# Two more y pairs in the key sweep, seven products in three more w2 steps, and another planned order

## The chip, the cores and the metric

The kernel runs on one core of a Trainium2 chip. The metric is the device time of one execution in microseconds (us); lower is better.

## The reference

What is computed, for `x` of 2048 rows by 576 columns (the second block's `B_x` has the same values as `A_x`):

```python
def _A_ref(x, wqkv, wo):                      # linear attention, 32 heads of 18 columns
    q, k, v = split_heads(x @ wqkv)
    phi = lambda t: where(t > 0, t + 1, exp(t)) + 1e-6
    pq, pk = phi(q), phi(k)
    kv = einsum("bhsd,bhse->bhde", pk, v);  z = pk summed over s
    o = (pq @ kv) / (pq . z + 1e-6)
    return merge_heads(o) @ wo

def _B_ref(x, w1, b1, w2, b2):                # 576 -> 4608 -> 576
    y = _layernorm(x, axis=-1)
    h = _gelu(y @ w1 + b1)
    return h @ w2 + b2

g = _sigmoid((x * gate_w).sum(-1, keepdims=True))
return g * _A_ref(x, ...) + (1 - g) * _B_ref(x, ...)
```

All data is float32. The kernel makes each product from a rounded high part and a low part of its operands (three terms: high by high, high by low, low by high).

## The kernel before

The program has three stages, one behind the other on TensorE (PE): a key sweep, the attention, and the two-layer block (called the MLP here).

**Key sweep.** The 2048 rows are 16 tiles of 128, taken in the order `ORDER`; the loop is `for n in range(FIRST, NT)`, and one turn of it is called round n here (3 to 15). In a round PE projects a tile's keys in two halves, into PSUM banks 6 and 7 (`project(i, KEY, half)`), adds the part `add_products(before, 0)` for the tile before, projects the queries in two halves into banks 6 and 7 again (`projected(i, QUERY)`), and adds the part `add_products(before, 1)`. The last three rounds (13 to 15) leave out the queries; those of the first of the three (`late[0]`) come behind the loop. A bank is free again when ScalarE (ACT) has made relu and exp of it (`e<-ps`, `e<-e`) and VectorE (DVE) has put both together: `k<-ps,e` for keys, `acc<-ps,e` (or `accs<-ps,e`) for queries. DVE also makes the low parts: `y<-t,y` for the next tile, `ks<-k,ks` and `xs<-xn,xs` for the sums. These instructions stand in program order on each engine.

**Slots and jobs.** Each round has three slots, 3n, 3n+1 and 3n+2, in which `run(slot)` puts other work into the same in-order queues: slot 3n stands behind `xs<-xn,xs` and ahead of the queries' `acc<-ps,e`, slots 3n+1 and 3n+2 behind these. Two kinds of jobs matter here:

- Gates and moments: in one slot DVE takes the row sums of two tiles (`gates_in`), in the next ACT takes exp and square root (`gates_act`, with two table loads), in the third DVE makes gate and 1/deviation in eight small instructions (`gates_out`) and GpSimd's queue (POOL) writes the two tiles' moments to DRAM (`share_moments`, in the profile `moments<-mr`).
- y pairs: the normalized x of two tiles, with the sums that seven products in place of eight need. `load_pair` reads the pair's moments back, spread over all partitions (`accs<-moments`), and x (`accs<-in_xm`, `accs<-in_xe`), seven issues on SyncE's queue (SP). Four `normal_pair` (`accs<-accs`, 768 wide), four `sum_pair` (384 wide), and four parts of `split_pair` and `split_tails` (an ACT copy, then two DVE instructions, `ys<-...`, the last part `y<-accs,y`) follow, and `store_pair` writes the parts to DRAM (`yd<-ys`). All pairs use one place, `yr` and `rows` in the tile `accs`: a pair is loaded over the one before.

`Y_JOBS` has the slots of each pair: that of the load, of the four normalizations, of the four differences, of the four parts. Before, the first half's four pairs are made so. The second half's four are made in the MLP (`make_y`, tiles `accs` and `ystage`).

**MLP.** The second half's rows follow the first's; each has 18 chunks of 256 of the 4608 columns, so there are 36 steps k. A step has "up" products (y by w1, seven products of seven matmuls, 512 wide) and "down" products (h by w2, 288 wide). For a step in `SEVEN` down is seven products, in 14 units of 6 matmuls; for another it is eight units of 12. Before, steps 0, 6, 13 and 35 are plain. A step in `SEVEN` costs sums ahead of its products: four of h (`u<-u`, 512 wide), four of w2 (`fresh<-fresh`, 288 wide), on DVE or POOL as the set `ON_DVE` says, more low parts (`h<-u,h`, `region<-fresh,region`), and more additions of products to the result (`accs<-ps,accs`).

The order of the MLP's instructions comes from `plan`, which takes each engine's next instruction by due times and costs written into it: `lag`, `late`, `slop` and other numbers of `TUNED`, a duration for each operation, and for PE one duration for every up matmul and one for every down matmul.

## Time and profile before

| | |
|---|---|
| median of 3 runs | 1095.46 us (1095.13 to 1095.92) |
| span of the profiled execution, first to last instruction | 1094.1 us |
| key sweep, up to the sums' last product | 0 to 180.6 us |
| attention | 180.6 to 272.6 us |
| MLP | 272.6 us to the end |
| PE, DVE, ACT, POOL busy | 1087.8, 917.2, 687.5, 235.6 us |

The profile has no time of its own for the profiled execution: its span is 1.36 us below the median of the runs, which also holds what lies ahead of the first and behind the last instruction. All shares are of the span. Nearly all instructions have the line L120, that of the helper which keeps program order, so one goes by tiles and shapes. A matmul's recorded duration holds the way through the array, so that durations of matmuls that follow each other overlap; their rate is read from how many start in a stretch of time. DVE's overlap too, by some 0.08 us each.

### The profile page before, as it was taken

How to read it: one execution, taken by the hardware profiler on the slowest of the kernel's cores; microseconds unless marked ns; L12 is line 12 of the kernel's file. 1: busy time of each engine (PE TensorE's matmuls, PEld its weight loads, DVE VectorE, ACT ScalarE, POOL GpSimd, SP SyncE). 2: the span in 40 equal slices, each digit the busy share in tenths (PEclk: the TensorE clock that was granted, in tenths of full speed). 3: DMA queues.
4: the chain of work that ended last, by engine and by line, in shares of the span. 5: the costliest groups of instructions: out<-in, count | busy, mean ns of one | idle time of the engine just before them, and what ended most of it. 6: DMA issues, size and time to landing. Idle time of an engine off the chain costs nothing.

```text
span 1094.1 us, 18599 instructions
## 1 busy us (share of the span) xinstructions
PE 1087.8 (99%) x6694; PEld 996.8 (91%) x6694; DVE 917.2 (84%) x1553; ACT 687.5 (63%) x1230; POOL 235.6 (22%) x232
## 2 busy tenths in 40 slices
PE   9999999999999999999999999999999999999998
PEld 9999999999898889988889999989899999999898
DVE  4568784895799999899999997988887888878888
ACT  6677765454667887777877876455545555455552
POOL 2111112531123232332111202121122211221110
PEclk9999999999999999999999999999999999999999
DMA  6466772745745565764556559574444435444432
GB/s 186 128 88 190 171 218 102 286 173 188 252 152 195 184 206 192 235 215 161 199 174 222 195 192 395 174 253 119 138 145 118 130 119 150 132 119 119 135 100 87
DMA packets 109006, 189.72 MB, mean 173 GB/s; under 512 B 8940, under 2 KB 68604, under 8 KB 104818
## 3 DMA queue, kind: packets, MB, share of 16 engines
q1 hardware_dynamic: 108002, 187.78, 53.3%
q8 instruction: 53, 0.87, 0.3%
q10 hardware_dynamic: 720, 0.74, 0.2%
q14 instruction: 39, 0.32, 0.1%
q0 software_dynamic: 192, 0.01, 0.1%
HBM read 121.70 MB, written 66.80 MB: 172 GB/s over the span
## 4 chain that ended last, share of the span: by engine, by line
PE 93%; DVE 3%; DMA 1%; ACT 1%; issue 0%; SPq 0%; ACTq 0%; DVEq 0%
PE ps L120 93%; DVE accs L120 1%; DMA s<-in_wm 0%; DVE h L120 0%; DMA fresh<-in_ue 0%; DMA ystage<-late_acc 0%; ACT u L120 0%; DMA s<-in_we 0%; DVE wp L120 0%; DVE region L120 0%; SPq L120 0%; DVE den L120 0%; DVE fresh L120 0%; DVE ystage L120 0%; DVE u L120 0%
## 5 line engine op out<-in xcount | busy, mean ns | idle before, releaser
L120 PEld LDWEIGHTS ps<-region,h 128*128 128x128 f32 x3072 | 437.8, 188 | 30.1 <-ACT ps L120 4.3
L120 PE MATMUL ps<-region,h 128*128 128x288 f32 x3072 | 457.1, 296 | 1.0 <-DVE region L120 0.4
L120 DVE TENSOR_TENSOR accs<-ps,accs 128x576 f32<-128x576 f32 x330 | 246.1, 753 | 60.9 <-PE ps L120 54.1
L120 PE MATMUL ps<-y,wa 128*128 128x512 f32 x1008 | 257.6, 393 | 0.0
L120 PEld LDWEIGHTS ps<-y,wa 128*128 128x128 f32 x1008 | 180.9, 188 | 30.3 <-ACT ps L120 0.2
L120 POOL TENSOR_TENSOR fresh<-fresh 128x288 f32<-128x288 f32 (+1 forms) x128 | 116.4, 913 | 410.5 <-DMA fresh<-in_w 129.6
L120 PE MATMUL ps<-y,wb 128*128 128x512 f32 x756 | 199.3, 394 | 0.1
L120 DVE TENSOR_TENSOR h<-u,h 128x512 fp32r<-128x512 f32 x240 | 165.9, 704 | 8.7 <-ACT u L120 8.7
L120 PEld LDWEIGHTS ps<-y,wb 128*128 128x128 f32 x756 | 133.9, 188 | 20.9 <-ACT u L120 0.5
L120 ACT ACTIVATE region<-fresh 128x576 fp32r<-128x576 f32 (+1 forms) x132 | 81.3, 625 | 73.5 <-PE ps L120 72.9
L120 PE MATMUL ps<-y 128*128 128x288 f32 (+1 forms) x896 | 125.8, 297 | 0.3 <-DVE y L120 0.2
L120 PEld LDWEIGHTS ps<-y 128*128 128x128 f32 x896 | 122.6, 189 | 1.8 <-DVE y L120 0.4
L120 ACT ACTIVATE ps<-ps 128x576 f32<-128x576 f32 (+1 forms) x127 | 78.7, 621 | 45.0 <-PE ps L120 21.5
L120 POOL TENSOR_TENSOR u<-u 128x512 f32<-128x512 f32 x44 | 57.0, 1296 | 193.5 <-DVE h L120 54.9
L120 DVE TENSOR_TENSOR region<-fresh,region 128x576 fp32r<-128x576 f32 (+1 forms) x132 | 93.8, 723 | 1.1 <-ACT region L120 1.1
L120 ACT ACTIVATE u<-ps 128x512 f32<-128x512 f32 x73 | 43.0, 589 | 68.4 <-PE ps L120 68.2
L120 ACT ACTIVATE h<-u 128x512 fp32r<-128x512 f32 x128 | 73.5, 622 | 10.0 <-DVE u L120 5.5
L120 ACT ACTIVATE h<-u,b1s 128x512 fp32r<-128x512 f32 x73 | 52.6, 722 | 42.6 <-DVE u L120 42.4
L120 PE MATMUL ps<-wp,qt 128*128 128x288 f32 x448 | 63.0, 297 | 0.0
L120 DVE TENSOR_TENSOR u<-ps,u 128x512 f32<-128x512 f32 x74 | 50.4, 683 | 13.5 <-PE ps L120 12.7
L120 PEld LDWEIGHTS ps<-wp,qt 128*128 128x128 f32 x448 | 59.8, 188 | 0.0
L120 DVE TENSOR_TENSOR u<-u 128x512 f32<-128x512 f32 x84 | 58.1, 691 | 1.7 <-POOL u L120 1.1
(137 smaller groups left out, 1052.1 us busy)
## 6 DMA issues: line engine op xcount, KB each, us to landing
w1d<-wa SPq DMA_DIRECT2D x17, 1280.0 KB
wa<-w1d SPq DMA_DIRECT2D x68, 320.0 KB
fresh<-in_w SPq DMA_DIRECT2D x70, 288.0 KB
y<-yd SPq DMA_DIRECT2D x14, 1280.0 KB
w1d<-wb SPq DMA_DIRECT2D x17, 960.0 KB
wb<-w1d SPq DMA_DIRECT2D x51, 320.0 KB
yd<-ystage SPq DMA_DIRECT2D x28, 320.0 KB
fresh<-in_um SPq DMA_DIRECT2D x64, 128.0 KB
```

The source lines that it names most:

```text
L120: self.last = self.tc.keep_in_program_order(op(*args, **kwargs))
```

## The change

Four things change.

1. `Y_JOBS` has six pairs: the first half's four, and two of the second half. `load_pair` and the others go to the right half by `divmod(pair, TPB)`. Pairs come every six slots: loads in slots 12, 18, 24, 30, 36 and 41. `MOMENTS` has groups of two tiles up to 12, with `GATES_AT` for their slots. Loads stand behind the other jobs of their slot. The last pair's jobs reach slot 48, behind the loop, and `run(48)` to `run(50)` stand between the last projections and products. `make_y` makes two pairs instead of four.
2. Steps 0, 6 and 13 are in `SEVEN`; step 13 is also in `FIVES`.
3. `ON_DVE` names each sum by itself, and `DVE_SUMS` is gone.
4. `plan` costs matmuls by their place in a run of the same kind (`EACH`), may hold a run of up products up to `hold` matmuls, and has other numbers in `TUNED`.

```diff
-MOMENTS = ((0, 2), (2, 4), (4, 6), (6, 8), (8, 16))
+MOMENTS = ((0, 2), (2, 4), (4, 6), (6, 8), (8, 10), (10, 12), (12, 16))
-Y_JOBS = ((13, (16, 16, 17, 17), (18, 18, 19, 19), (18, 19, 20, 21)), (20, (22, 22, 23, 23), (25, 25, 27, 27), (25, 26, 28, 29)), (27, (31, 31, 32, 32), (33, 33, 34, 34), (34, 35, 35, 36)), (35, (37, 37, 38, 38), (39, 39, 41, 41), (40, 42, 43, 44)))
+Y_JOBS = ((12, (15, 15, 16, 16), (16, 17, 17, 18), (17, 18, 19, 20)), (18, (21, 21, 22, 22), (22, 23, 23, 24), (23, 24, 25, 26)), (24, (27, 27, 28, 28), (28, 29, 29, 30), (29, 30, 31, 32)), (30, (33, 33, 34, 34), (34, 35, 35, 36), (35, 36, 37, 38)), (36, (39, 39, 40, 40), (40, 41, 41, 42), (41, 42, 43, 44)), (41, (44, 44, 45, 45), (45, 46, 46, 47), (46, 47, 47, 48)))
+GATES_AT = (9, 13, 19, 25, 31, 37)
-SEVEN = set([1, 2, 3, 4, 5, 7, 8, ...
+SEVEN = set([0, 1, 2, 3, 4, 5, 6, 7, 8, ...
-    for b, n in enumerate((9, 13, 22, 28)):
+    for b, n in enumerate(GATES_AT):
...
-    for j, (loaded, normal, added, parts) in enumerate(Y_JOBS):
-        at(loaded, load_pair, 0, j)
+    for pair, (loaded, normal, added, parts) in enumerate(Y_JOBS):
+        sup, j = divmod(pair, TPB)
         for n, when in enumerate(normal):
...
+    for pair, (loaded, *_) in enumerate(Y_JOBS):
+        at(loaded, load_pair, *divmod(pair, TPB))
...
     projected(late[0], QUERY)
+    run(3 * NT)
     queries_out(late[0])
     moments_of(end)
+    run(3 * NT + 1)
     for part in range(2):
         add_products(end, part)
+    run(3 * NT + 2)
...
+    EACH = {"up": (226.8, (6.3, 9.3, -2.7, 4.3, 9.3, 1.5, 5.5, 4.2)), "down": (131.9, (0, 3, -1, -2, 7, 1, 2, 3, -6, 1, 0, 1))}
...
-        own = ((what, k, m) in ON_DVE) != ((m, k < NCHUNK) in DVE_SUMS)
+        own = (what, k, m) in ON_DVE
...
-        for j in range(TPB):
+        for j in range(len(Y_JOBS) - TPB, TPB):
             dma(lambda j=j: load_pair(1, j), raw_free["rows"], [("yraw", j)], 5600, 7, each=700)
...
-                        if tb <= ta + 100:
+                        if tb <= ta + 100 and not (run[0] == "up" and run[1] < hold and behind < wait and ta <= free[PE]):
```

What this does to the order, at three places. First DVE in round 11, from the end of the low parts to the queries of the round. Before: two differences (384 wide) stand ahead of the two `acc_101<-ps,e` that free banks 6 and 7.

```order
L120 SCALAR_TENSOR_TENSOR k<-ps,e 128x288
L120 SCALAR_TENSOR_TENSOR ks<-k,ks 128x576
L120 TENSOR_TENSOR xs<-xn,xs 128x512
L120 TENSOR_TENSOR xs<-xn,xs 128x64
L120 TENSOR_TENSOR accs<-accs 128x384 x2
L120 SCALAR_TENSOR_TENSOR acc_101<-ps,e 128x288 x2
L120 TENSOR_TENSOR accs<-accs 128x384 x2
```

The same place now, where the eight instructions of `gates_out` are followed by two normalizations:

```order
L120 TENSOR_TENSOR xs<-xn,xs 128x64
L120 TENSOR_SCALAR g<-g 128x2
L120 RECIPROCAL g<-g 128x2
L120 TENSOR_SCALAR omg<-g 128x2
L120 RECIPROCAL mr_114<-mr_114 128x2
L120 TENSOR_TENSOR mt<-mr_114 128x2
L120 TENSOR_TENSOR mt<-mt 128x2
L120 TENSOR_SCALAR mt<-mt 128x2
L120 TENSOR_TENSOR mr_114<-mr_114,mt 128x2
L120 TENSOR_TENSOR accs<-accs 128x768 x2
L120 SCALAR_TENSOR_TENSOR acc_101<-ps,e 128x288 x2
L120 TENSOR_TENSOR accs<-accs 128x768 x2
```

Gates and normalizations of one round now meet ahead of the queries' instructions; rounds 5, 7 and 9 have the same form.

Second, DVE at the end of the sweep, rounds 14 and 15. Before, from the low parts of round 14 on (`ys` and `y` are parts of the fourth pair, the row `k<-ps,e x2` is the keys of round 15):

```order
L120 TENSOR_TENSOR xs<-xn,xs 128x64
L120 TENSOR_TENSOR ys_561<-accs,ys_561 128x2x256
L120 SCALAR_TENSOR_TENSOR ys_561<-ys_561,low_rows,accs 128x2x128
L120 TENSOR_TENSOR ys_562<-accs,ys_562 128x2x256
L120 SCALAR_TENSOR_TENSOR ys_562<-ys_562,low_rows,accs 128x2x128
L120 TENSOR_TENSOR y<-accs,y 128x256
L120 SCALAR_TENSOR_TENSOR y<-y,low_rows,accs 128x128
L120 SCALAR_TENSOR_TENSOR k<-ps,e 128x288 x2
L120 SCALAR_TENSOR_TENSOR ks<-k,ks 128x576
L120 TENSOR_TENSOR xs<-xn,xs 128x512
L120 TENSOR_TENSOR xs<-xn,xs 128x64
L120 SCALAR_TENSOR_TENSOR acc_102<-ps,e 128x288 x2
```

Now the same stretch holds the fourth difference and three parts of the fifth pair, and the first two normalizations of the sixth, ahead of the keys of round 15:

```order
L120 TENSOR_TENSOR accs<-accs 128x384
L120 TENSOR_TENSOR ys_565<-accs,ys_565 128x2x256
L120 SCALAR_TENSOR_TENSOR ys_565<-ys_565,low_rows,accs 128x2x128
L120 TENSOR_TENSOR ys_566<-accs,ys_566 128x2x256
L120 SCALAR_TENSOR_TENSOR ys_566<-ys_566,low_rows,accs 128x2x128
L120 TENSOR_TENSOR y<-accs,y 128x256
L120 SCALAR_TENSOR_TENSOR y<-y,low_rows,accs 128x128
L120 TENSOR_TENSOR accs<-accs 128x768 x2
L120 SCALAR_TENSOR_TENSOR k<-ps,e 128x288 x2
L120 SCALAR_TENSOR_TENSOR ks<-k,ks 128x576
L120 TENSOR_TENSOR xs<-xn,xs 128x512
L120 TENSOR_TENSOR xs<-xn,xs 128x64
```

And between these low parts and `acc_102<-ps,e`, the queries behind the loop, which stood next to each other, there are now the rest of the sixth pair's jobs:

```order
L120 TENSOR_TENSOR accs<-accs 128x768 x2
L120 TENSOR_TENSOR accs<-accs 128x384 x3
L120 TENSOR_TENSOR ys_564<-accs,ys_564 128x2x256
L120 SCALAR_TENSOR_TENSOR ys_564<-ys_564,low_rows,accs 128x2x128
L120 TENSOR_TENSOR accs<-accs 128x384
L120 TENSOR_TENSOR ys_565<-accs,ys_565 128x2x256
L120 SCALAR_TENSOR_TENSOR ys_565<-ys_565,low_rows,accs 128x2x128
L120 TENSOR_TENSOR ys_566<-accs,ys_566 128x2x256
L120 SCALAR_TENSOR_TENSOR ys_566<-ys_566,low_rows,accs 128x2x128
L120 TENSOR_TENSOR y<-accs,y 128x256
L120 SCALAR_TENSOR_TENSOR y<-y,low_rows,accs 128x128
L120 SCALAR_TENSOR_TENSOR acc_102<-ps,e 128x288 x2
```

Third, PE where the down products begin (step 0, `ps<-region,h`, between up products `ps<-y,wa` and `ps<-y,wb`). Before:

```order
L120 MATMUL ps<-y,wa 128x512 x28
L120 MATMUL ps<-region,h 128x288 x12
L120 MATMUL ps<-y,wb 128x512 x7
L120 MATMUL ps<-region,h 128x288 x24
L120 MATMUL ps<-y,wb 128x512 x7
```

Now:

```order
L120 MATMUL ps<-y,wa 128x512 x28
L120 MATMUL ps<-y,wb 128x512 x4
L120 MATMUL ps<-region,h 128x288 x6
L120 MATMUL ps<-y,wb 128x512 x3
L120 MATMUL ps<-region,h 128x288 x6
L120 MATMUL ps<-y,wb 128x512 x11
```

Step 0's units are of 6 matmuls now. Over the whole MLP the down matmuls go from 3072 to 3036, and the runs of up matmuls between them from 298 to 281.

More of the change, by code (lines that the diff above doesn't have):

```diff
@@ L557, in tile_gated_mix @@
     y_stages.append(y_place.rearrange("p (m s n) -> p m s n", m=2, s=5))
-    jobs = {n: [] for n in range(3 * NT)}
+    jobs = {n: [] for n in range(3 * NT + 3)}
     def at(n, f, *args):
@@ L1418, in tile_gated_mix, with plan @@
     assert len(in_order) == len(ops)
-    def plan(lag, late, slop, slack, guard, ahead, second=None):
-        second = second or (lag, late, slop, slack, guard, ahead)
+    def plan(lag, late, slop, slack, guard, ahead, second, hold, wait):
         slot, due = {o: n for n, o in enumerate(ups)}, {}
@@ L1444, in plan, with streams @@
         port_at, moved, landed = {e: 0 for e in port_until}, 0.0, []
-        next_up, next_down, shift = 0, 0, 0.0
+        next_up, next_down, shift, run = 0, 0, 0.0, ["", 0]
+        def streams(o):
+            n = round(o.ns / (231.7 if o.by[0] == "up" else 132.3))
+            each, more = EACH[o.by[0]]
+            at_ = run[1] if run[0] == o.by[0] else 0
+            return n, n * each + sum(more[at_:at_ + n])
         def offer(o):
@@ L1523, in plan @@
             s, _, o = min(picks, key=lambda x: x[:2])
-            e, t = o.engine, s + o.tail
+            e, t, ns = o.engine, s + o.tail, o.ns
             if e == PE:
+                n, ns = streams(o)
+                t += ns - o.ns
+                run[:] = o.by[0], n + (run[1] if run[0] == o.by[0] else 0)
                 shift = s - nominal[o]
@@ L1530, in plan @@
                         late, slop, slack, guard = second[1:5]
+                        hold, wait = second[6:8]
                 else:
@@ L1553, in plan @@
             else:
-                free[e] = s + o.ns
+                free[e] = s + ns
             if o.port:
```

23 lines of the change are left out of this document (11 added, 12 removed).

## The prediction

> **What bounds the kernel now.** The page comes first: span, busy time, chain.
>
> ```profile
> span 1094.1 us, 18599 instructions
> ...
> PE 1087.8 (99%) x6694; PEld 996.8 (91%) x6694; DVE 917.2 (84%) x1553; ACT 687.5 (63%) x1230; POOL 235.6 (22%) x232
> ...
> PE 93%; DVE 3%; DMA 1%; ACT 1%; issue 0%; SPq 0%; ACTq 0%; DVEq 0%
> ```
>
> PE is busy 1087.8 of 1094.1 us and makes 93% of the chain. What the change takes from PE's work comes off the time, unless PE starts to wait for something that now hides under it. So the next view is busy time by stretch: rounds 10, 12 and 14 of the key sweep, and the tail from the late queries to the sums' last product. Columns: stretch, its length, then busy us (and instructions) of PE, PE's weight loads, DVE, ACT and POOL, the granted clock, the DMA share, GB/s.
>
> ```profile
> 117.12:128.32 11.20, 11.20 (x77) 10.76 (x75) 7.24 (x21) 9.29 (x21) 1.78 (x2) 1.00 0.85 254
> ...
> 139.52:150.72 11.20, 11.20 (x77) 10.76 (x75) 9.03 (x20) 7.89 (x18) 1.44 (x1) 1.00 0.82 217
> ...
> 158.20:165.68 7.48, 7.48 (x49) 7.05 (x47) 6.57 (x14) 5.20 (x13) 1.44 (x1) 1.00 0.70 222
> ...
> 173.16:180.61 7.45, 7.45 (x48) 7.03 (x47) 3.46 (x9) 2.47 (x6) 0.00 (x0) 1.00 0.00 2
> ```
>
> PE is busy for the whole of each stretch: a full round takes 11.20 us, one without queries 7.48. DVE works 6.6 to 9.0 us of these, so it has room on the average, but it works in order, and PE's next step needs certain DVE instructions at certain times. PE's own rows give the two times that matter at the sweep's end: the late queries begin at 173.16, the sums' product at 180.61.
>
> ```profile
> 165.68 3.90 PE L120 MATMUL ps<-y 128*128 128x288 f32 x28
> ...
> 173.16 3.88 PE L120 MATMUL ps<-y 128*128 128x288 f32 x28
> ...
> 180.61 1.13 PE L120 MATMUL ps<-pks,ones 128*128 128x288 f32 x4
> ```
>
> In a full round, PE's next keys need bank 6 back, which is the first `acc<-ps,e` of the queries. Round 10 (from 117.12) shows how near that is. Columns: start, time taken, operation; a count at the end joins neighbours.
>
> ```profile
> 125.52 0.82 DVE L120 TENSOR_TENSOR xs<-xn,xs 128x512 fp32r<-128x512 f32 x2
> 126.26 0.16 DVE L120 TENSOR_SCALAR g<-g 128x2 f32<-128x2 f32 x1
> ...
> 127.52 0.16 DVE L120 TENSOR_TENSOR mr<-mr,mt 128x2 f32<-128x2 f32 x1
> 127.59 0.82 DVE L120 SCALAR_TENSOR_TENSOR acc<-ps,e 128x288 f32<-128x288 f32 x2
> 128.33 3.80 DVE L120 TENSOR_TENSOR accs<-accs 128x768 f32<-128x768 f32 x4
> ```
>
> The low parts `xs` end at 126.34, 9.2 us after the round's start; `gates_out` takes 1.33 us (126.26 to 127.59), and the first `acc<-ps,e` ends some 0.46 us later, 128.05. The next round starts at 128.32: 0.27 us are left. The four normalizations of this round (3.80 us, 0.95 each) stand behind the queries.
>
> **Part 1: the jobs of rounds 5, 7, 9 and 11.** Now `gates_out` and two normalizations meet ahead of the queries' `acc<-ps,e`. Where `xs` ends without pair work ahead of it is seen in round 12, with the sweep's end behind it:
>
> ```profile
> 147.08 0.81 DVE L120 TENSOR_TENSOR xs<-xn,xs 128x512 fp32r<-128x512 f32 x2
> ...
> 157.12 1.23 DVE L120 SCALAR_TENSOR_TENSOR ks<-k,ks 128x576 fp32r<-128x576 f32 x1 [0.96 <-ACT ks L120]
> 158.27 0.81 DVE L120 TENSOR_TENSOR xs<-xn,xs 128x512 fp32r<-128x512 f32 x2
> 159.00 1.14 DVE L120 TENSOR_TENSOR accs<-accs 128x384 f32<-128x384 f32 x2
> 160.06 0.68 DVE L120 TENSOR_TENSOR ys<-accs,ys 128x512 fp32r<-128x512 f32 x1
> 160.66 0.48 DVE L120 SCALAR_TENSOR_TENSOR ys<-ys,low_rows,accs 128x256 fp32r<-128x256 f32 x1
> 161.06 1.14 DVE L120 TENSOR_TENSOR accs<-accs 128x384 f32<-128x384 f32 x2
> ```
>
> Round 12 starts at 139.52 and its `xs` ends at 147.89, 8.4 us on. Round 5 has no pair work of the round before ahead of it, so it is like that: 8.4 + 1.3 + 1.9 + 0.46 = 12.1 us, and PE wants the bank at 11.2: 0.9 late. Rounds 7, 9 and 11 have a pair's last part ahead, as round 10 had: 9.2 + 1.3 + 1.9 + 0.46 = 12.8, 1.6 late each. Sum 0.9 + 3 x 1.6 = 5.7 us. At the lower end the low parts come no later than in round 12 everywhere and it is 3.6; if ACT's two further pairs of table loads come on top, up to 7. I take 5.7, since the round with the same work ahead gave 9.2. Rounds 6, 8, 10 and 12 hold a difference (0.57) and a part (1.0) there: 9.2 + 1.6 + 0.46 = 11.3 at worst, against 11.2; I add nothing.
>
> **Part 2: the sixth pair.** Its moments and load are next; the rows are the write of moments (median from issue to landing at the end), a pair's load on SP's queue, and a load and the instruction that waited for it.
>
> ```profile
> moments<-mr POOLq DMA_DIRECT2D x4, 2.0 KB, 10.6
> ...
> 138.61 0.33 SPq L120 DMA_DIRECT2D accs<-moments  x1
> 140.79 0.58 SPq L120 DMA_DIRECT2D accs<-in_xm  x1
> ...
> 143.41 1.12 SPq L120 DMA_DIRECT2D accs<-in_xe  x2
> ...
> 265.74 0.56 SPq L120 DMA_DIRECT2D accs<-in_ue  x1
> ...
> 269.86 2.10 POOL L120 TENSOR_TENSOR accs<-accs 128x384 f32<-128x384 f32 x2 [21.81 <-DMA accs<-in_ue]
> ```
>
> Rounds 13, 14 and 15 now begin 5.7 later, at 156.4, 163.9 and 171.4. `gates_out` of the sixth pair's tiles stands in slot 39, ends at 156.4 + 9.2 + 1.3 = 166.9, and POOL writes the moments at 167.0. They land 10.6 us later, 177.6. SP waits for that, then issues seven transfers at 0.56 to 0.58 each, the last at 181.2. A load issued at 265.74 was there for its reader at 269.86, 4.1 us later; so all has landed at 185.3. Queued behind on SP are the low copy of x for round 15 and the stores `yd<-ys`; nobody waits for these next.
>
> Who waits is seen from the order: the load stands in slot 41, and the fifth pair's fourth difference and last three parts in slots 42 to 44 read places that the load writes. They wait for it, and being in order they hold up everything behind them on ACT and DVE: the `e<-ps` and `k<-ps,e` of round 15. From 185.3: ACT's copy of a part 0.83, then DVE's two instructions for two parts (0.6 + 0.4 each, from 160.06 to 161.06), 2.0, the small part 0.6, two normalizations 1.9, and the first `k<-ps,e` 0.46: bank 6 is free at 191.1. PE would be ready for the late queries at 173.16 + 5.7 = 178.9, and waits up to 12 us, whole or in part already at round 15's keys; the sum needs only that the bank comes at 191.1.
>
> Behind that the queue goes on: second `k<-ps,e` 0.4, the wait of `ks` for ACT 0.96 (row 157.12), `ks` 1.15, `xs` 0.75, two normalizations 1.9, three differences 1.7 (0.57 each), a part 1.0, the fourth difference 0.5, two parts 2.0, the small one 0.6, and only then `accs<-ps,e` of the late queries, 0.46. Sum 11.4: 202.5. The sums' product needs that bank. PE meanwhile makes the queries (3.9 us from 191.1) and the last products (3.6, from 173.16 to 180.61 less the queries), is done at 198.6 and waits a second time, 4 us. The sums' product moves from 180.61 to 202.5, +21.8 us with part 1 in it. Everything after it is the same attention, so this goes to the end in full.
>
> The DMA price is the widest. If the moments landed at once, the load would still wait until DVE has done the reads ahead of it, about 9.2 us into round 14 (173.1), and have landed at 173.1 + 3.6 + 4.1 = 180.8: 4.5 us less. The trace's 10.6 us is the median of four such writes from this queue in this same sweep, so I take it. The Trainium skill, "DMA: Bandwidth & Descriptors", section "Anatomy of one DMA — SWDGE (gpsimd) path", puts a transfer from that queue at about 2.0 us plus its bytes; by it the sweep would lose 4.5 us less and the total be an estimated 1108, but the trace's 10.6 us for 2 KB contradicts it here.
>
> **Part 3: the MLP.** Rows: PE in a stretch of down products alone; the clock behind the last matmul; the first half.
>
> ```profile
> 1076.00:1088.00 12.00, 12.00 (x92) 1.00 0.27 100
> ...
> 1092.60:1094.10 1.50, 0.00 (x0) 0.50 0.00 0
> ...
> 294.00:646.00 352.00, 351.21 (x2078) 315.37 (x2078) 338.25 (x566) 270.72 (x448) 87.92 (x82) 1.00 0.56 192
> ```
>
> 92 down matmuls start in 12 us: 12/91 = 0.132 us each. There are 3072 - 3036 = 36 fewer, -4.75 us. Seventeen fewer changes between up and down products, at a hundredth of a microsecond, -0.2. In return DVE and POOL get work, priced by these groups (columns: instructions, busy us, mean ns, idle before):
>
> ```profile
> L120 DVE TENSOR_TENSOR accs<-ps,accs 128x576 f32<-128x576 f32 x330 | 246.1, 753 | 60.9 <-PE ps L120 54.1 <-ACT u L120 3.4
> L120 DVE TENSOR_TENSOR h<-u,h 128x512 fp32r<-128x512 f32 x240 | 165.9, 704 | 8.7 <-ACT u L120 8.7
> L120 DVE TENSOR_TENSOR region<-fresh,region 128x576 fp32r<-128x576 f32 x101 | 79.8, 792 | 1.1 <-ACT region L120 1.1
> L120 DVE TENSOR_TENSOR u<-u 128x512 f32<-128x512 f32 x84 | 58.1, 691 | 1.7 <-POOL u L120 1.1
> ...
> L120 DVE TENSOR_TENSOR accs<-accs 128x768 f32<-128x768 f32 x32 | 29.9, 951 | 0.4
> ...
> L120 DVE TENSOR_TENSOR accs<-accs 128x384 f32<-128x384 f32 x32 | 18.5, 577 | 0.3
> ...
> L120 DVE TENSOR_TENSOR fresh<-fresh 128x288 f32<-128x288 f32 x32 | 15.4, 480 | 0.0
> ...
> L120 DVE TENSOR_TENSOR ystage<-accs,ystage 128x256 fp32r<-128x256 f32 x28 | 11.7, 416 | 0.0
> L120 DVE SCALAR_TENSOR_TENSOR ystage<-ystage,low_rows,accs 128x128 fp32r<-128x128 f32 x28 | 11.0, 394 | 2.6 <-ACT ystage L120 2.6
> ```
>
> In the first half DVE gains 14 evictions (10.5 us), 9 low parts of h (6.3), three of w2 at 792 and three at about 480 (3.8), and with the new sharing 4 sums of h (2.8), 5 of w2 (2.4), 3 of w1 (577, 1.7): 27.5. It loses two y pairs: 8 x 951 + 8 x 577 + 14 x (416 + 394) = 23.6. Net +3.9 us. In 294 to 646 DVE is busy 338.25 of 352.00, so it would be at 342 of 347; PE still has more. I cost this at nothing: PE hides it, with 5 us of room; if that is gone, see the third rival. The y pairs' loads leave SP's queue there too, which can only help. The new due times I also cost at nothing either way: PE is busy 351.21 of 352.00 before, so better order can give at most 0.8 in this stretch.
>
> **Sum.** 1094.1 + 21.8 - 4.75 - 0.2 = 1110.95 of span; outside the span lie 1095.46 - 1094.1 = 1.36 us; 1112.3, forecast 1112.
>
> **Rivals.**
>
> *The clock falls at the second wait.* The row from 1092.60 has a granted clock of 0.50, about 2 us after the last matmul. The first wait (10 us or more) is long enough for that; queries and products at half rate would take up to 3.9 us more, which is just the second wait, so it costs nothing. But the second wait of 4 us would then end with attention at half rate: 1 to 5 us, take 2.5: about 1115. The Trainium skill, "TensorE: Matmul & The Clock Gate", Part 1, says that the clock comes back only after some 3.4 us of busy matmuls; by it, half that time is lost at each return. The row at the end agrees that it falls; no row here shows how it comes back in the middle of the kernel.
>
> *The sweep loses less.* Part 1 absorbed (DVE waits less where it starts late): 21.8 - 5.7 = 16.1, 1106.5. Or the moments land quickly: 4.5 less, 1108.
>
> *DVE becomes the bound in the MLP.* If DVE can't use its 13.75 us of idle time in 294:646, since it waits there for products, the stretch would take 352 + 3.9 in place of 352 - 4.8: 8.7 more at worst, 1121; half of it 1116.5. For it: 96% busy. Against: most idle ahead of `accs<-ps,accs` is released by PE.
>
> *The sweep hides the pairs: faster.* DVE has 2 to 4 us free in each round, and if the last load landed before its readers' turn, only 4.95 us of PE's work would be left to count: 1090.5. This decides at one place: the load must be there by about 174, when the fifth pair's fourth difference has its turn, some 7 us after `gates_out` ends at 166.9. The rows say 10.6 + 3.6 + 4.1 = 18.3 us. Part 1 must vanish too.
>
> *Nothing changes:* gain and loss would have to be equal, a loss in the sweep of 5 us.
>
> **How the numbers follow.** The sum as worked out has 0.55 (1109 to 1114.5); the clock 0.15 (about 1115); a smaller loss 0.14 (1106 to 1108); DVE in the MLP 0.06 (1116.5 to 1121); hidden 0.08 (1090.5); equal 0.02. The range 1103.5 to 1118 holds the first three, 0.84 with a share of the fourth, and takes in the ends of part 1 and of the moments together (1112.3 - 2.1 - 4.5 = 1105.7; 1112.3 + 1.3 and the clock's 2.5 to 4: 1118). Faster by over 0.2%: 0.08; within 0.2% (2.2 us, about what a measurement of this kernel can tell from no change): 0.02; slower: 0.90.
>
> **What the profile after would show.** The sums' product `ps<-pks,ones` begins at about 202 and not 181; PE waits 0.9 to 1.6 us at the ends of rounds 5, 7, 9 and 11 for DVE; 10 to 12 us idle on PE ahead of the late queries, with DVE and ACT idle until the sixth load (`accs<-in_xe`) has landed at about 185; a second idle time of about 4 us before the sums' product. From there to the end the length falls by 5 us, from 913.5 to about 908.5, with PE as busy as before. A granted clock below 1.00 behind 202 shows the first rival, DVE without idle time in the MLP's first half and PE below 99% there the third. The forecast is wrong if the moments' write lands in 2 to 4 us, if the last pair's readers don't wait for its load, or if rounds 5 to 11 keep 11.2 us.

## The result and the profile after

The changed kernel takes 1123.85 us (median of 4 runs, 1123.2 to 1124.49) against 1095.69: ratio 1.0252, 95% interval 1.024 to 1.0264. It is slower by 28.2 us, where 16.5 were forecast, and lies 5.9 us above the range.

The page of the changed kernel:

```profile
span 1121.5 us, 18636 instructions
...
PE 1091.6 (97%) x6658; PEld 994.6 (89%) x6658; DVE 957.6 (85%) x1612; ACT 703.6 (63%) x1249; POOL 252.0 (22%) x238
...
PE 71%; DVE 4%; DMA 3%; ACT 1%; issue 1%; SPq 0%; DVEq 0%; ACTq 0%
```

PE's work is 3.8 us more than before (1091.6 for 1087.8), although it has 36 matmuls less: matmuls at a lower clock count as busy for longer (28 of them 5.54, 5.24 and 6.69 us for 3.9 in three of the rows below). 29.9 us of the span are without PE work; PE's share of the chain falls from 93% to 71%. PE's rows show where (start, duration, operation, count; in brackets the idle time ahead and what ended it). Each is the beginning of a round's keys, or of the late queries (200.40), the last is the sums' product:

```profile
61.71 3.90 PE L120 MATMUL ps<-y 128*128 128x288 f32 x28
...
74.30 4.00 PE L120 MATMUL ps<-y 128*128 128x288 f32 x28 [1.22 <-DVE accs L120]
...
85.67 4.01 PE L120 MATMUL ps<-y 128*128 128x288 f32 x28
...
99.30 5.54 PE L120 MATMUL ps<-y 128*128 128x288 f32 x28 [2.04 <-DVE accs L120]
...
125.05 4.00 PE L120 MATMUL ps<-y 128*128 128x288 f32 x28 [1.55 <-DVE acc L120]
...
150.04 4.00 PE L120 MATMUL ps<-y 128*128 128x288 f32 x28 [2.08 <-DVE acc L120]
...
161.41 4.00 PE L120 MATMUL ps<-y 128*128 128x288 f32 x28
...
179.77 5.24 PE L120 MATMUL ps<-y 128*128 128x288 f32 x28 [3.14 <-DVE k L120]
...
200.40 6.69 PE L120 MATMUL ps<-y 128*128 128x288 f32 x28 [11.64 <-DVE k L120]
...
211.83 1.21 PE L120 MATMUL ps<-pks,ones 128*128 128x288 f32 x4 [0.96 <-DVE acc L120]
```

The losses stand in four places. From the program's start to round 5 the two executions differ by 0.6 us (61.71 for 61.12). Rounds 5 to 12 take 99.7 us (61.71 to 161.41) for 89.6: 10.1 more. From round 13 to the late queries it is 38.99 (161.41 to 200.40) for 22.44: 16.55 more. From there to the sums' product 11.43 for 7.45: 4.0 more. Together the sums' product comes 31.2 us later (211.83 for 180.61). From it to the end the kernel takes 909.7 us for 913.5: 3.8 less.

Stretches of the same kernel (columns as in the prediction: round 7, round 8, round 15 with its wait, and the MLP's first half):

```profile
85.67:99.30 13.63, 11.59 (x77) 10.61 (x76) 9.46 (x27) 9.80 (x22) 2.20 (x2) 1.00 0.92 289
99.30:112.14 12.84, 12.84 (x75) 12.40 (x76) 11.11 (x24) 8.13 (x19) 1.42 (x1) 0.87 0.37 81
179.77:200.40 20.63, 8.99 (x48) 8.21 (x48) 8.66 (x17) 5.69 (x13) 1.41 (x1) 0.75 0.51 153
...
304.00:690.00 386.00, 385.49 (x2239) 343.15 (x2238) 375.12 (x605) 298.76 (x494) 105.70 (x103) 1.00 0.55 186
```

In round 8 (99.30) the granted clock is 0.87, and DVE works 11.11 of 12.84 us. In the stretch of 179.77 to 200.40, which is round 15 and the wait behind it, no engine is busy for half of the time. In the MLP's first half PE is busy 385.49 of 386.00 us.

### The profile page after: what moved, and what is told of

The parts are those of the page before. It is cut to its first block, busy times and chain, and to the rows that moved or that the text cites. A ratio compares the mean times of both kernels' runs of the same rounds, so it can differ in the third digit from the quotient of the medians.

```text
span 1121.5 us, 18636 instructions
## 1 busy us (share of the span) xinstructions
PE 1091.6 (97%) x6658; PEld 994.6 (89%) x6658; DVE 957.6 (85%) x1612; ACT 703.6 (63%) x1249; POOL 252.0 (22%) x238
## 4 chain that ended last, share of the span: by engine, by line
PE 71%; DVE 4%; DMA 3%; ACT 1%; issue 1%; SPq 0%; DVEq 0%; ACTq 0%
PE ps L120 71%; DMA y<-yd 1%; DVE accs L120 1%; DMA accs<-late_acc 1%; DVE h L120 1%; DMA fresh<-in_ue 1%; DMA fresh<-in_w 1%; SPq L120 0%; ACT h L120 0%; DMA yd<-ystage 0%; DVE u L120 0%; DVE region L120 0%; DVE wa L120 0%; ACT ps L120 0%; DVE wp L120 0%
## 5 line engine op out<-in xcount | busy, mean ns | idle before, releaser
L120 PEld LDWEIGHTS ps<-region,h 128*128 128x128 f32 x3036 | 430.3, 188 | 30.2 <-ACT ps L120 5.1
L120 PE MATMUL ps<-region,h 128*128 128x288 f32 x3036 | 449.6, 295 | 0.6 <-ACT ps L120 0.4
L120 DVE TENSOR_TENSOR accs<-ps,accs 128x576 f32<-128x576 f32 x344 | 252.6, 752 | 37.6 <-PE ps L120 32.6
L120 DVE TENSOR_TENSOR h<-u,h 128x512 fp32r<-128x512 f32 x249 | 179.1, 746 | 10.2 <-ACT u L120 9.9
L120 POOL TENSOR_TENSOR u<-u 128x512 f32<-128x512 f32 x73 | 98.0, 1343 | 286.7 <-DVE h L120 108.9
L120 POOL TENSOR_TENSOR fresh<-fresh 128x288 f32<-128x288 f32 (+1 forms) x103 | 90.0, 877 | 299.0 <-DVE h L120 89.1
L120 PE MATMUL ps<-y 128*128 128x288 f32 (+1 forms) x896 | 132.4, 306 | 23.0 <-DVE k L120 14.8
L120 PEld LDWEIGHTS ps<-y,wb 128*128 128x128 f32 x756 | 133.9, 188 | 21.6 <-issue 0.6
L120 ACT ACTIVATE ps<-ps 128x512 f32<-128x512 f32 (+1 forms) x135 | 84.0, 624 | 56.6 <-PE ps L120 37.6
L120 ACT ACTIVATE h<-u 128x512 fp32r<-128x512 f32 x140 | 82.0, 620 | 5.7 <-DVE u L120 3.9
L120 DVE TENSOR_TENSOR accs<-accs 128x768 f32<-128x768 f32 (+1 forms) x64 | 49.0, 766 | 9.5 <-DMA accs<-in_xe 8.2
```

Source lines behind the costliest of these rows:

```text
L120: self.last = self.tc.keep_in_program_order(op(*args, **kwargs))
```

## The experiments

In a table first; the times are medians, each compared with runs of the kernel before on the same chip.

| kernel | us | ratio to before, 95% interval | sums' product at, us |
|---|---|---|---|
| changed | 1123.85 | 1.024 to 1.0264 | 211.8 |
| e1_old_sweep | 1121.89 | 1.0219 to 1.0247 | 182.0 |
| e2_new_sweep | 1126.43 | 1.0262 to 1.029 | 211.0 |
| e3_five_pairs | 1115.75 | 1.017 to 1.0198 | 193.8 |
| e4_load_42 | 1118.58 | 1.0189 to 1.0217 | 207.6 |
| e5_share_sp | 1126.40 | 1.0254 to 1.0291 | 216.0 |
| e6_normals_behind | 1123.00 | 1.0228 to 1.026 | 210.3 |
| e7_gates_early | 1129.48 | 1.0286 to 1.0338 | 216.8 |
| e8_seven_only | 1131.06 | 1.0303 to 1.0335 | 182.7 |
| e9_half_normals | 1115.95 | 1.016 to 1.019 | 205.1 |
| e10_no_sixth_write | 1115.32 | 1.0156 to 1.019 | 204.3 |
| e11_write_later | 1121.49 | 1.0216 to 1.0247 | 210.3 |
| e12_old_sweep_light | 1121.09 | 1.0203 to 1.0249 | 181.0 |
| e13_new_order | 1105.11 | 1.0062 to 1.0096 | 181.7 |

### Sweep or MLP: e1, e2, e3

```diff
 e1_old_sweep, against the changed kernel
-MOMENTS = ... (6, 8), (8, 10), (10, 12), (12, 16))
+MOMENTS = ... (6, 8), (8, 16))
+Y_JOBS = (the four pairs of before)
-GATES_AT = (9, 13, 19, 25, 31, 37)
+GATES_AT = (9, 13, 22, 28)
```

> The changed kernel with the key sweep of before (its Y_JOBS, gates and groups of moments: four pairs in the sweep, four in the MLP); SEVEN, ON_DVE and the planner stay as changed. Theory 1 (all of the loss is made in the sweep, and the MLP gains by itself): 1095.7 - 3.8 = 1091.9 us, since from the sums' product to the end the changed kernel took 909.7 us against 913.5. Theory 2 (the seven products in steps 0, 6 and 13 need the two pairs out of the MLP, DVE being near its limit there): DVE gets 23.6 us back in the first half, where it had 11 us of idle time (375.1 busy of 386.0), so up to 12 us later: 1093 to 1104 us, with DVE busy over 98% from 304 to 690.

Measured 1121.89 us. The sweep's loss was gone (sums' product at 182.0), and the MLP was 31 us longer than in the changed kernel (940.9 us from there to the end in the profiled execution, which took 1124.65 us; by the medians it is 28 us). Neither number fits: the loss is larger than the missing room on DVE. This is taken up again with e8, e12 and e13.

```diff
 e2_new_sweep, against the kernel before
 + Y_JOBS, GATES_AT, MOMENTS, run(48) to run(50), make_y of the changed kernel
```

> The kernel before with the changed key sweep alone (six pairs there, two in the MLP); SEVEN, ON_DVE and the planner as before. Theory 1: the sums' product at about 211.8 us as in the changed kernel, and the MLP as before less nothing: 1095.7 + 31.2 = 1126.9 us. Rival (PE waits in the MLP for DVE, 4.2 us in all, and two pairs fewer there take those waits away): down to 1122.7 us.

1126.43 us, the sums' product at 211.0, and 913.3 us from there to the end, as before. So the sweep's loss belongs to the new sweep alone, and two pairs fewer in the old MLP bring nothing.

```diff
 e3_five_pairs, against the changed kernel
-Y_JOBS = (..., (36, ...), (41, ...))
+Y_JOBS = (..., (36, ...))
-GATES_AT = (9, 13, 19, 25, 31, 37)
+GATES_AT = (9, 13, 19, 25, 31)
```

> The changed kernel without the sixth pair in the sweep: five pairs there, three in the MLP. Theory 1 (two separate losses: 10.1 us in rounds 5 to 12, 21.1 us by the sixth pair's load, which the queue of DVE and ACT waits for): the sums' product at 180.6 + 10.1 = 190.7 us, and 1123.9 - 21.1 = 1102.8 us. Rival (DVE has too much work in the sweep, and each of the two new pairs costs the like): half of the loss, 15.6 us, goes: 1108.3 us. In both the MLP may lose up to 1 us by the third pair.

1115.75 us. The sweep did nearly what theory 1 said: the sums' product at 193.8 (190.7 expected), 18.0 us earlier. But the MLP with a third pair took 923.3 us in the profiled execution, 13.6 more than the changed one, and not up to 1. That execution (1118.91 us) lies 3.2 us above the median, so by the medians it is some 10 us. I had taken the MLP for free there too.

### Rounds 5 to 12: e6 and e9

```diff
 e6_normals_behind, against the changed kernel (first four pairs)
-(15, 15, 16, 16) (21, 21, 22, 22) (27, 27, 28, 28) (33, 33, 34, 34)
+(16, 16, 16, 16) (22, 22, 22, 22) (28, 28, 28, 28) (34, 34, 34, 34)
```

> The changed kernel with the first two normalizations of the first four pairs one slot later (16, 22, 28, 34 for 15, 21, 27, 33), behind the queries' acc<-ps,e. Theory A, that of the prediction (two normalizations, 1.95 us, stand ahead of the instruction that frees bank 6, and this sets the loss of each round): each of the four losses of 1.4 to 2.4 us gets smaller by up to 1.95: 7 us less, and the 1.6 us of the halved clock go too: about 1115.5 us. Theory B (DVE and ACT have no idle time from gates_in to the keys' instructions of the next round, so that the time is set by the sum of their work and not by its order): PE begins the next keys earlier and waits ahead of the next queries instead: 1123.9 us, or 1122 if the clock stays up with the shorter waits.

1123.00 us: theory B. PE's rows of the keys of round 8, its queries, and the keys of round 10 (start, duration, idle time ahead):

```profile
97.61 4.00 PE L120 MATMUL ps<-y 128*128 128x288 f32 x28
...
104.83 3.97 PE L120 MATMUL ps<-y 128*128 128x288 f32 x28 [1.47 <-DVE k L120]
...
122.50 4.00 PE L120 MATMUL ps<-y 128*128 128x288 f32 x28
```

The wait ahead of the keys has become one of 1.47 us ahead of the queries, where bank 6 must be freed by the keys' `k<-ps,e`. Two rounds (97.61 to 122.50) take 24.9 us, as in the changed kernel (125.05 to 150.04: 25.0). Only the order had changed.

```diff
 e9_half_normals, against the changed kernel
     def normal_pair(sup, j, a, k):
+        if sup == 0 and k == 1:
+            return
```

> The changed kernel without the second of each two normalizations (the multiplication) of the first four pairs: 8 instructions of 0.95 us left out, one ahead of the queries' acc<-ps,e and one behind it in each pair's rounds. Theory A (in rounds 5 to 12 DVE's work as a whole, with what it must wait for ACT, is longer than PE's: two rounds take 24.9 to 25.8 us where PE needs 22.4): each two rounds get shorter by the 1.9 us that DVE has less, 4 x 1.9 = 7.6 us, and the halved clock of round 8 (1.6) goes with the shorter waits: 1114.7 to 1116.3 us. Theory B (only what stands ahead of acc<-ps,e counts): 4 x 0.95 = 3.8 us, 1120.1 us. Theory C (ACT's table loads set the loss): 1123.9 us.

1115.95 us, theory A. The keys of rounds 6, 8 and 10:

```profile
73.68 4.01 PE L120 MATMUL ps<-y 128*128 128x288 f32 x28 [0.22 <-DVE accs L120]
...
96.96 4.01 PE L120 MATMUL ps<-y 128*128 128x288 f32 x28 [0.61 <-DVE accs L120]
...
120.17 4.01 PE L120 MATMUL ps<-y 128*128 128x288 f32 x28 [0.55 <-DVE acc L120]
```

Two rounds now take 23.2 to 23.3 us for 25.0 to 25.8: 1.7 us less or more, where DVE has 1.9 us less to do. Rounds 5 to 12 lose because DVE, with the waits for ACT that its order holds, has more to do than PE: a pair now comes every two rounds, where before there was one every seven or eight slots. Rounds 11 and 12 of the changed kernel show it (the stretch, then what DVE waits for in it: us, times, longest):

```profile
136.42:161.41 24.99, 22.91 (x151) 21.27 (x151) 19.83 (x46) 17.89 (x39) 3.62 (x3) 1.00 0.64 186
...
DVE y L120 <- ACT y L120: 2.7, 1, 2.7
DVE ks L120 <- ACT ks L120: 1.8, 2, 1.0
```

DVE is busy 19.83 of 24.99 us and waits 4.7 us for ACT (a third wait is 0.2 us), and never for PE.

### The sixth pair: e4, e10, e5

The chain in the changed kernel, on POOL, SP, DVE and ACT; the last row is a stretch, with DMA share and GB/s at its end:

```profile
172.94 0.77 POOL L120 DMA_DIRECT2D moments<-mr  x1 [3.00 <-DVE mr L120]
...
185.00 0.36 SPq L120 DMA_DIRECT2D accs<-moments  x1
...
187.96 1.85 SPq L120 DMA_DIRECT2D accs<-in_xe  x2
...
192.01 0.56 DVE L120 TENSOR_TENSOR accs<-accs 128x384 f32<-128x384 f32 x1 [8.23 <-DMA accs<-in_xe]
...
199.89 0.82 DVE L120 SCALAR_TENSOR_TENSOR k<-ps,e 128x288 f32<-128x288 f32 x2
...
194.55 1.58 ACT L120 ACTIVATE ys<-accs 128x768 fp32r<-128x768 f32 x2 [12.32 <-DMA accs<-in_xe]
...
178.00:185.00 7.00, 5.23 (x29) 5.26 (x30) 4.94 (x10) 1.89 (x4) 1.41 (x1) 0.76 0.03 4
```

The write is issued at 172.94, the load's first transfer at 185.00 (12.06 us later), its last two from 187.96; DVE's fourth difference has what it needs at 192.01, ACT's copy of a part, which reads the last transfers, at 194.55; `k<-ps,e` follows at 199.89, PE at 200.40. In the last 7 us of the 12 the queues move 4 GB/s: most of this time is not transfer, and what passes in it the trace doesn't show.

```diff
 e4_load_42, against the changed kernel
-(41, (44, 44, 45, 45), ...)
+(42, (44, 44, 45, 45), ...)
```

> The changed kernel with the load of the sixth pair one slot later (42 for 41), behind the fifth pair's fourth difference and second part, so that these and the parts after them don't wait for it. The load is issued at the same time, since it waits for the moments (issued 172.94, read from 185.00). Theory 1: the first instructions that wait are then the two first normalizations, which need four of the seven transfers, landed at about 189.8; keys' bank free at 189.8 + 1.9 + 0.5 = 192.2 and not 200.4, 8.2 us earlier: 1115.7 us. Rival (whatever waits first, the whole queue stands until all seven have landed at 192.0): 192.0 + 1.9 + 0.5 = 194.4, 6 us earlier: 1117.9 us. If the wait on PE is not by this load at all: 1123.9 us.

```profile
186.42 0.33 SPq L120 DMA_DIRECT2D accs<-moments  x1
...
193.81 1.95 DVE L120 TENSOR_TENSOR accs<-accs 128x768 f32<-128x768 f32 x2 [5.66 <-DMA accs<-in_xe]
...
196.18 6.50 PE L120 MATMUL ps<-y 128*128 128x288 f32 x28 [6.97 <-DVE k L120]
```

1118.58 us, 5.3 less; the late queries began at 196.18, 4.2 earlier. The two normalizations were the first to wait, as theory 1 said, but the load began 1.4 us later (186.42 for 185.00) and the first transfers were there only at 193.81, 7.4 us after its start, so that the rival's 194.4 for the late queries is the nearer number. What waits first is worth 4 us; whether the write makes the rest is the question of e10.

```diff
 e10_no_sixth_write, against the changed kernel
     def share_moments(b):
+        if b == 5:
+            return
 (load_pair: the sixth pair reads the fifth pair's moments)
```

> The changed kernel without the write of the sixth pair's moments; its load reads the fifth pair's in their place (so the sixth pair is normalized with wrong numbers) and waits for no write. The write was issued at 172.94 and read from 185.00 in the changed kernel, 172.61 and 184.25 with SP's queue. Theory A (the load waits for that write, and all from the load to the sums' product waits for the load): the load starts when its place has been read, at 179.3, 5.7 us earlier: 1123.9 - 5.7 = 1118.2 us, or a little less, as no write is under way meanwhile. Theory B (the load is late for another reason, x or a store ahead of it on SP): 1123.9 us.

```profile
176.54 0.36 SPq L120 DMA_DIRECT2D accs<-moments  x1
...
181.43 1.11 SPq L120 DMA_DIRECT2D accs<-in_xe  x2
...
192.85 5.51 PE L120 MATMUL ps<-y 128*128 128x288 f32 x28 [3.81 <-DVE k L120]
```

1115.32 us: theory A. The load starts at 176.54 for 185.00, as soon as the first of its places is free, its last two transfers go out from 181.43 for 187.96, 6.5 us earlier, the late queries begin at 192.85, 7.5 earlier, and the time falls by 8.5. That is more than the 5.7 expected: x's transfers begin 6.5 us earlier (178.92 for 185.45), are issued in 3.6 us for 4.4 and are there 0.3 us sooner behind the last issue. The other 0.8 us lie between the profiled executions (7.7 us apart in span) and the medians.

```diff
 e5_share_sp, against the changed kernel
-        pool.dma_start(moments[b]...
+        (sp if b == 5 else pool).dma_start(moments[b]...
```

> The changed kernel with the sixth pair's moments written by SP's queue and not by POOL's; the slots are the same. In the changed kernel this write was issued at 172.94 us, and what reads it at 185.00. Theory A (the 12 us are a cost of POOL's queue): on SP the write lands within some 3 us, the load then waits for the reads ahead of it only, which end at 179.3, and everything from the load on comes 5.7 us earlier: 1123.9 - 5.7 = 1118.2 us. Theory B (a write of 512 pieces of 4 bytes takes this long from any queue): 1123.9 us, and if SP's queue stands meanwhile, its loads and stores are late too: up to 1126.

```profile
172.61 0.36 SPq L120 DMA_DIRECT2D moments<-mr  x1
...
184.25 0.36 SPq L120 DMA_DIRECT2D accs<-moments  x1
```

1126.40 us, theory B: from SP's queue the write was issued at 172.61 and its reader went on at 184.25, 11.6 us later. The Trainium skill, "SBUF — State Buffer", section "Who interferes with whom", says that a transfer of POOL's queue that seems held up by DVE is short of descriptors, and that this disappears with another queue. Here it stayed (11.6 us for 12.06): it isn't POOL's queue but the write. The kernel is 2.5 us slower than the changed one, as the load took longer: one issue on SP took 3.94 us (from 186.94), and the last two transfers left from 191.32 for 187.96. Why that issue took so long is not shown.

### The write holds up others: e7 and e11

```diff
 e7_gates_early, against the changed kernel
-GATES_AT = (9, 13, 19, 25, 31, 37)
+GATES_AT = (9, 12, 18, 24, 30, 37)
```

> The changed kernel with the gates of the second to fifth pair of tiles one slot earlier (12, 18, 24, 30 for 13, 19, 25, 31), so that ACT's two table loads (3.2 us with what belongs to them) stand ahead of the second part's products and not right ahead of the next keys' e<-ps, and gates_out stands at the end of the even round and not with the normalizations. Theory A (in the changed kernel ACT's gates_act, which waits for gates_in, holds up the keys' e<-ps by 1.2 to 2 us in rounds 5, 7, 9 and 11, and all of DVE behind it): the loss of rounds 5 to 12 falls from 10.1 to about 4 us, and the halved clock of round 8 with it: 1123.9 - 6 to 7.6 = 1116.3 to 1117.9 us. Theory B (only normalizations and gates_out ahead of acc<-ps,e count, as in the prediction): gates_out goes, 1.4 us in each of four rounds: 1123.9 - 5.6 = 1118.3 us; the rows of ACT then tell them apart: by A the first e<-ps of round 7's keys comes 2 us after the round's start, by B still 4 us after it. If table loads in even rounds hold up the queries instead: 1123.9 us.

1129.48 us: slower, which no theory had. The first pair's load and the write of the next moments (POOL, SP, DVE; then stretches with DMA share and GB/s in the last columns):

```profile
64.22 0.78 POOL L120 DMA_DIRECT2D moments<-mr  x1 [6.17 <-DVE mr L120]
...
63.74 0.34 SPq L120 DMA_DIRECT2D accs<-moments  x1
...
66.75 2.22 SPq L120 DMA_DIRECT2D accs<-in_xe  x2
...
76.91 1.95 DVE L120 TENSOR_TENSOR accs<-accs 128x768 f32<-128x768 f32 x2 [6.30 <-DMA accs<-in_xe]
...
67.00:70.00 3.00, 3.00 (x23) 2.90 (x22) 1.82 (x3) 2.39 (x8) 1.42 (x1) 1.00 0.84 203
70.00:73.00 3.00, 3.00 (x22) 2.91 (x21) 0.61 (x2) 1.51 (x4) 0.00 (x0) 1.00 0.88 33
73.00:76.50 3.50, 0.60 (x3) 0.21 (x2) 0.00 (x0) 0.00 (x0) 0.00 (x0) 1.00 0.80 63
```

The write went out at 64.22 among the transfers of the load (63.74 to 69), and these were there at 76.91; in the 6.5 us ahead of that the queues moved 33 to 63 GB/s, with 203 in the 3 us before. PE waited 5.7 us. From round 8 on two rounds took 24.1 to 25.3 us, so the place of the gates brought nothing there either.

```diff
 e11_write_later, against e7_gates_early
-        at(n + 2, share_moments, b)
+        at(n + (3 if n % 6 == 0 else 2), share_moments, b)
```

> The kernel with the gates a slot earlier (1129.5 us), with the moments' write of those four groups one slot later, where it was in the changed kernel. With the early write PE waited 5.7 us in round 5 for the first pair's load: seven transfers issued at 63.7 to 69 us were only there at 76.9, the write having been issued at 64.2; in the changed kernel transfers issued at 63.0 to 68.6 were there before 71.9, the write being issued at 72.1. Theory A (a write of 512 pieces of 4 bytes keeps other transfers waiting for some 10 us): the load is there in time, and the wait of round 5 goes: 1129.5 - 5 to 7 = 1122.5 to 1124.5 us. Theory B (the load was late for other reasons): 1129.5 us.

1121.49 us, 8.0 less than e7 and 1.0 below the range of theory A, and the wait of round 5 was gone (0.75 us left). That a write of 512 pieces keeps other transfers waiting is shown by these two; why it does is not.

### Four pairs in the MLP: e8, e12, e13

```diff
 e8_seven_only, against the kernel before
-SEVEN = set([1, 2, 3, 4, 5, 7, ... 12, 14, ...
+SEVEN = set([0, 1, 2, 3, 4, 5, 6, 7, ... 12, 13, 14, ...
 (with the changed kernel's ON_DVE, FIVES, and sums named one by one)
```

> The kernel before (four pairs in the sweep, four in the MLP, its planner and its numbers) with steps 0, 6 and 13 as seven products and the new ON_DVE alone. The changed kernel with the old sweep took 1121.9 us: its MLP was 27 us longer than that of before. Theory A (DVE hasn't the room for the sums and evictions of three more steps beside four y pairs): here too PE waits between 400 and 690 us: 1110 to 1125 us. Theory B (the numbers of the planner, made for two pairs in the MLP, give a bad order with four): with the old numbers the loss is gone, 1091 to 1098 us.

1131.06 us, 6.1 above A's range; the sums' product at 182.7 as it should. So with four pairs in the MLP the three steps lose with the old numbers as well as with the new.

```diff
 e12_old_sweep_light, against e1_old_sweep
-                op(DVE, lambda j=j, n=n: normal_pair(1, j, n // 2, n % 2), ...
+                op(DVE, lambda: None, ...
-                op(DVE, lambda j=j, n=n: sum_pair(1, j, n), ...
+                op(DVE, lambda: None, ...
```

> The changed kernel with the sweep of before (1121.9 us) and without the normalizations and differences of the four pairs in the MLP: 32 DVE instructions, 24.4 us, left out; the order of all others, ACT's copies, the low parts and all transfers stay. Theory A (the MLP of that kernel was 31 us longer since DVE had no room for four pairs beside the new sums): the MLP is as in the changed kernel, 909.7 us from the sums' product, and the time 1093 to 1096 us. Theory B (ACT's copies, SP's transfers or the order made the loss): 1115 to 1122 us.

The stretch 300 to 700 us of the changed kernel, of e1_old_sweep with what PE waits for, of e12_old_sweep_light, and of e13_new_order, which follows (columns as above: PE, PE's loads, DVE, ACT, POOL, clock):

```profile
300.00:700.00 400.00, 399.49 (x2330) 356.35 (x2330) 382.36 (x619) 305.85 (x505) 110.76 (x107) 1.00 0.57 192
```

```profile
300.00:700.00 400.00, 383.48 (x2174) 336.82 (x2173) 379.49 (x630) 290.17 (x486) 104.30 (x100) 0.98 0.55 190
...
PE ps L120 <- ACT ps L120: 7.7, 9, 1.4
PE ps L120 <- DVE h L120: 4.0, 3, 1.7
```

```profile
300.00:700.00 400.00, 383.66 (x2182) 337.82 (x2181) 360.36 (x600) 291.52 (x488) 103.52 (x100) 0.98 0.56 192
```

```profile
300.00:700.00 400.00, 391.79 (x2282) 345.79 (x2281) 390.83 (x647) 301.62 (x503) 110.55 (x108) 1.00 0.60 207
```

1121.09 us: theory A, that DVE's work as such makes the loss, falls. DVE has 19 us less in this stretch (360.36 for 379.49), and PE is busy no more than in e1_old_sweep (383.66 for 383.48). In the changed kernel DVE has as much to do (382.36) and PE waits for half a microsecond. So it is the order, or something else than DVE.

A part of the loss is the clock, which falls behind PE's waits. In e1_old_sweep the granted clock is 0.72 to 0.83 in four stretches of 9 to 12 us (457 to 466, 556 to 568, 586 to 596, 638 to 648). That makes some 17 us at half the clock, and an estimated 8.5 us of loss beside the 16.5 us in which PE is idle. e12_old_sweep_light has 17 us of it too.

```diff
 e13_new_order, against e1_old_sweep: the same work, shared and ordered in another way
-ON_DVE = ..., TUNED = ... (found for two pairs in the MLP)
+ON_DVE = ..., TUNED = ... (searched for four pairs, by the planner's costs)
```

> The changed kernel with the sweep of before (four pairs in the sweep, four in the MLP; 1121.9 us), with a new ON_DVE and new numbers of the planner, searched for four pairs by the planner's own costs. By these costs PE's last product ends at 839.3 us in the order of that kernel, at 810.5 in the changed kernel, at 816.9 in the kernel before, and at 823.7 in the best order that the search found. Theory A (the loss with four pairs in the MLP is made by an order whose numbers were found for two pairs, and the chip follows the planner's costs): 15.6 us of the 31 us come back: 1121.9 - 15.6 = 1106.3 us, still slower than before. Theory B (the chip lacks room on DVE whatever the order): 1115 to 1122 us.

1105.11 us: theory A, 16.8 us back for 15.6 expected. PE is idle 8.2 us of the stretch (row above) for 16.5, and the clock stays at 1.00: about half of the gain is waiting that is gone, and, by the estimate above, half is the clock that no longer falls. The planner's costs hold no clock, so that the two numbers agree so well is in part luck. Sharing of the sums between DVE and POOL and order together are more than half of what e1 lost; they were not changed one by one. The rest (922.4 us from the sums' product, 8.9 more than before) stands in the best order found, and whether a better one exists is open. No kernel of these was faster than the one before.

## Why the prediction was wrong, point by point

**The direction was right, the mechanism in the main, and two sizes failed by about the same: part 1 by 4.4 us and part 2 by 4.3.** The change is slower by the sweep; PE waits ahead of the keys of rounds 6, 8, 10 and 12, and at the late queries for the sixth pair's load, and the MLP gains. From the late queries to the sums' product 11.4 us were forecast, 11.43 are there. The size was too small by 11.6 us (1123.85 for 1112.3), at these terms:

- **Part 1: 5.7 forecast, 10.1 measured.** The step "the round with the same work ahead gave 9.2" failed. It held in round 9 (9.2), but in rounds 7 and 11 `xs` ended 9.9 us after the round's start, since ACT's `gates_act`, late itself because it waits for `gates_in`, stood ahead of the keys' `e<-ps` (round 7, ACT's rows, then one of DVE):

```profile
86.44 1.28 ACT L120 ACT_TABLE_LOAD   x1
...
87.94 1.28 ACT L120 ACT_TABLE_LOAD   x1
...
89.76 0.39 ACT L120 ACTIVATE e<-ps 128x288 f32<-128x288 f32 x1
...
94.75 0.81 DVE L120 TENSOR_TENSOR xs<-xn,xs 128x512 fp32r<-128x512 f32 x2
```

The first three rows are ACT's two table loads and the keys' `e<-ps`, 4.1 us after round 7's start (85.67); the last is DVE's `xs`, which ends at 95.56. Round 5 gave 8.75 for 8.4. That 8.4 was read wrongly: round 12 of the kernel before is not without pair work (two differences and three parts stand ahead of its keys, from 139.02 to 143.1); what it lacks is `gates_act`, which round 10 has. So rounds 5, 7, 9 and 11 lost 8.0 us for 5.7.

Deeper, the step was wrong in kind: it took one instruction's place for the cause, and e6 shows that its place doesn't matter, e9 that the work in two rounds does. "I add nothing" for rounds 6, 8, 10 and 12 hid that DVE is behind in them and hands this on to the next round. They lost 2.1 us themselves, 1.5 of it by the clock in round 8 (below); of this round 9 gave 0.7 back, since DVE caught up meanwhile (it lost 1.7 us, round 7 2.4).

- **Part 2, to the late queries: 12.3 forecast (191.1 less 156.4, against 22.44), 16.55 measured.** `gates_out` later than planned in its round +0.9 (11.5 us after the start, planned 10.6); the write's landing +1.5 (12.06 for 10.6); the load +1.85 (9.55 us from its first issue to ACT's copy, planned 7.7, as the price of a transfer was 4.1, from the MLP, and 6.05 here, 188.5 to 194.55); from there on 5.85 for 5.8. All three are sizes, not a missing mechanism; e10 shows the write in the chain. The range couldn't hold them: its upper end, 1118, took in more for part 1 and for the clock, and nothing for a slower write or load. (202.5 less 180.61 is 21.9, not 21.8.)

- **Part 3: 4.95 forecast, 3.8 measured.** The 36 matmuls brought what was said: added up from start to start, down takes 404.8 us for 409.6. The up products take 408.8 for 407.9, 0.9 more where 0.2 less was forecast, in small waits at the change to down products. The hundredth of a microsecond for a change stands in no row of the prediction: in the trace before, an up matmul ahead of a down one takes 233.1 ns until the next starts, for 230.9 ahead of another up one, and a down matmul ahead of an up one 134.5 for 133.3. "I cost this at nothing" for DVE's 4 us was right in the result: the third rival, DVE as the bound, didn't happen here (PE 385.49 of 386.00). e1, e8 and e3 show that it is lost again with three or four pairs in the MLP; whether two pairs with the old order would have kept it was not run. The low parts of h became slower too, 746 ns for 704; POOL has more sums beside them (512 wide: 73 for 44), but that these are the cause is not shown:

```profile
L120 DVE TENSOR_TENSOR h<-u,h 128x512 fp32r<-128x512 f32 x249 | 179.1, 746 | 10.2 <-ACT u L120 9.9
```

- **The clock rival** came half. Behind the first wait the clock fell: the 28 matmuls of the late queries took 6.69 us for 3.88, hidden in the second wait as the prediction said. That wait was then 0.96 us for 4, and behind it the clock was 1.00 (212 to 220 us), so that attention lost nothing. It fell at two places that were not forecast: at the keys of round 15 (5.24 us, after a wait of 3.14), which cost nothing, as a longer wait follows, and in round 8, where 28 matmuls after a wait of 2.04 us took 5.54 for 4.0.

- 0.6 us more lie at the program's start, 1.0 us in the time outside the span and between the profiled run (1123.2) and the median.

**The rival "a smaller loss"** rested on quick landing; the trace's own 10.6 us was too low rather than too high. The faster rival named its condition rightly: the load had to be there some 7 us after `gates_out`, and came 21.6 us after the write was issued (172.94 to 194.55).

## What to carry to other kernels

Where engines are in-order and each round is nearly full, don't price one instruction's place: add up an engine's work, with the waits that its order holds, over the whole period in which the work repeats, and set it beside the period of the engine that bounds. Price a chain over DRAM from the slowest row of its own kind and place, write, wait and read each by itself. An order searched for one amount of work is no measure for another: before giving up a move, search its own order.

## What the runs showed of the hardware

- Writing 2 KB in pieces of 4 bytes takes about 12 us until a reader may go on, from POOL's queue (12.06) or SP's (11.6), in the changed kernel the last 7 of them with 4 GB/s on the queues, and other transfers issued among it are late by several us (e7 and e11). The Trainium skill, "DMA: Bandwidth & Descriptors", section "Anatomy of one DMA — SWDGE (gpsimd) path", has about 2.0 us fixed for a transfer; the runs disagree for this form.
- The clock can halve after a wait of 2 us, and need not: after 2.04 us 28 matmuls took 5.54 us (99.30), after 2.08 us 4.00 (150.04). In the first case it was 0.50 from 100.7 to 104.1. Shorter waits close together can do it too: in e1_old_sweep waits of 0.72, 1.66 and 0.38 us between 454.8 and 459.8 were followed by a clock of 0.81 from 457 to 466. The Trainium skill, "TensorE: Matmul & The Clock Gate", section "What's actually happening", has a free-running window of about 3.4 us, which fits that the same wait ends both ways; that a whole window must be idle, as its table says, doesn't fit 2.04 us.
